# Spectral mixing with a gated feed-forward on one core: moving a group of transfers from the sync engine to GpSimd, and one sum into a DMA

## The chip, the cores and the metric

The kernel runs on one core of a Trainium2 chip. TensorE (PE in the profile) multiplies; VectorE (DVE) and ScalarE (ACT) do elementwise work; GpSimd (POOL) and SyncE (SP) issue transfers here; 16 DMA engines move the data. Each engine runs its own instructions in order and waits on semaphores for the others. The metric is the device time of one execution in microseconds; for comparing two kernels the median of several runs is used.

## The reference

With xn the layer-normalised x (2048 tokens, 512 features), two things are computed and joined:

```
a = xn @ dft_hid_re.T;  b = xn @ dft_hid_im.T           # [2048, 512]
s = dft_seq_re @ a - dft_seq_im @ b                     # [2048, 512]
h = xn @ w1 + b1;  h = max(h, 0) ** 2                   # [2048, 1792]
g = silu(h @ w2 + b2)
out = x + s * g
```

All in float32. The two hidden DFT matrices are 512 x 512, the two sequence matrices 2048 x 2048.

## The kernel before, in words

**Arithmetic.** Every operand is split into a high part, which TensorE takes in its fast float32 format (F32R), and a low part, the rest. A product is three passes: high x high, high x low, low x high. `split_hi` (L138) is done on ScalarE, `split_lo` (L141) on VectorE. Larger products use a scheme of seven block products in place of eight (`PRODUCTS`), for which sums and differences of the four blocks of an operand are needed. An operand with its sums has seven blocks, in a high and a low part.

**Sequence part.** The sequence DFT is done first, on xn itself: two products, P and Q, of xn with the sequence matrices, in eight chunks c of 256 output tokens. The first chunk (L410) is done without the scheme while x is still being normalised, and so is the first tile of the second chunk, j = 4 (`MIXED`, `plain_step`). All other tiles go through `steps`: first (1, 1), (1, 0), (1, 3), (1, 2), (1, 5), (1, 6), (1, 7), then eight tiles j for each of the chunks 2 to 7. A step is 42 products on TensorE (L399). For a later step, `step_load` (L291) loads a raw tile of the sequence matrices, 512 KB in four blocks, into one of three buffers u; `step_sums` makes four more blocks of it on VectorE (`sums_b`: one addition of two blocks at L305, then one block each at L311 and L312); `step_split` splits seven blocks into the buffer ga or gb (by the parity of j). The load for the step after next but two is issued when its buffer u comes free.

For the first step's tile, (1, 1), the addition of L305 is not done on VectorE: the loop over the first chunk loads the two blocks a second time into the place of the sum (L594) and lets GpSimd issue an accumulating DMA that adds the third block to both (L595). `step_sums` then does only L311 and L312 (`sums_b_rest`).

xn needs the same sums, in place in its tiles xn32, for two groups of four tiles (`sums`, L270): three subtractions on VectorE for a whole group (L275) and, for each tile, one accumulating DMA of GpSimd (L278). `split_sums` puts the result into the operands XC (tile xc) just ahead of the steps that use them, in the order 1, 0, 3, 2, 5, 6, 7, 4.

**Work beside the steps.** When a chunk is done, `closing` combines its seven accumulators into a tile e (c in the transfers' names), and at the steps j = 3 and 4 of the following chunk P and Q are stored to DRAM (PQD, L667). The table `EARLY` lists by step what else is done: seven weights' jobs (`weight`: d0 to d3 for the hidden DFT, v0, v1 and v6 for blocks of w1). A job loads a raw weight into pq00 (L449), makes its sums in pq01, splits them and stores the seven blocks, high and low, to DRAM in two transfers (L462, to WDD or W1D). Four jobs `load_wd` (p1, p0, p3, p2 in that order) load the hidden DFT's operands back into SBUF when room is free there, each in two halves, high then low (L513, tile wdp). P and Q are read back by `y_load` and `y_early` (L469).

**Hidden part and the rest.** From WDP and the operands of P and Q, eight units (YUnit, tiles r_A to r_D, L807) make s; then w1 (HUnit, L807) and w2 (L913, tiles m_o and m_last), and at last the gate and the output.

**Queues.** The program's order is written out by hand; each engine follows it. Nearly all transfers, loads and stores, are issued by SP in one queue (q1 in the profile). ScalarE issues the stores of s and h (q10). GpSimd issues 16 accumulating transfers (q0): the one of L595, eight of L278, and seven of L951 in the last part, which add x to the output. An issue waits for its semaphores on the issuing engine, and what is behind it on that engine waits too.

Of the kernel before, what the change touches and what calls it, by code (L numbers as in the profile page):

```python
# [8 lines left out]
F32 = mybir.dt.float32  # L9
# [123 lines left out]
def fnet_gated_kernel(ctx, tc, x, xt, ct, wd, w1, w2, b1, b2, out):  # L133
    nc = tc.nc
    ctx.enter_context(tc.manual_schedule(engines=None))

    def split_hi(hi, lo, src):
        nc.scalar.activation(hi, src, AF.Copy)  # L138
# [4 lines left out]
    def split(*parts):  # L143
        split_hi(*parts)
        split_lo(*parts)

    def copy(to, src, scale=1.0):
        nc.scalar.activation(to, src, AF.Copy, scale=scale)
# [12 lines left out]
    PQD = [dram.tile([P, 2, 4, 256], F32, name=f"pqd{c}") for c in range(NC)]  # L161
    WDD = [dram.tile([P, 2, 7, 256], F32, name=f"wdd{n}") for n in range(ND)]
# [9 lines left out]
    def buf(tag, shape, name, dtype=F32):  # L172
        return pool.tile(shape, dtype, tag=tag, bufs=3 if tag == "u" else 1, name=name)
# [96 lines left out]
    def sums(g):  # L270


        s = xn32[ND * g, "tile"].rearrange("p j h (b n) -> p j (h b) n", b=2)
        for to, a, b in ((3, 1, 3), (1, 1, 0), (0, 3, 0)):
            nc.vector.tensor_tensor(s[:, :, to], s[:, :, a], s[:, :, b], op=ALU.subtract)  # L275
            yield
        for j in (1, 0, 3, 2):
            nc.gpsimd.dma_start(s[:, j, 2], s[:, j, 0], accum_op=ALU.add)  # L278
        yield

# [4 lines left out]
    raw, part = {}, {}  # L285
# [60 lines left out]
    def step_sums(n):  # L346
        if n < len(steps):
            u = raw[steps[n]]
            (sums_b if n else sums_b_rest)(u[:, 4:8], u)

    def step_split(n):
        if n < len(steps):
# [79 lines left out]
    steps = [(1, j) for j in SEVEN] + [(c, j) for c in range(2, NC) for j in range(NJ)]  # L432
    order = [(0, j) for j in range(NJ)] + [(1, j) for j in MIXED] + steps
# [12 lines left out]
    def weight(n, raw_, sums_, to, k, turn=False):  # L446

        r = buf("pq00", [P, 4, 256], f"{n}r")
        nc.sync.dma_start(r, raw_)  # L449
        yield  # L450
        t = buf("pq01", [P, 4, 256], f"{n}t")
        if turn:
            copy(r[:, I22:I21 + 1], r[:, I22:I21 + 1], -1.0)
        first = sums_(t, r)
        next(first)
        yield
        list(first)
        yield
        g = buf(f"wd{int(k)}", [P, 2, 7, 256], f"{n}g", F32R)
        for q, src in ((slice(0, 3), r[:, 1:4]), (slice(3, 7), t)):  # L460
            split(g[:, HI, q], g[:, LO, q], src)
            nc.sync.dma_start(to[:, :, q], g[:, :, q].bitcast(F32))  # L462
            yield

    makers["d"] = lambda n: weight(f"wd{n}", wd[n], sums_b_steps, WDD[n], n % 2, True)
# [43 lines left out]
    def load_wd(n):  # L509
        t = operand_buf(("wd0", "wd1", "xc2", "xc1")[n], f"wdp{n}", 0)  # L510
        WDP[n] = t
        for i in range(2):
            nc.sync.dma_start(t[:, i].bitcast(F32), WDD[n][:, i])  # L513
            yield

    makers["y"] = y_early
# [42 lines left out]
    g = plain_parts(0, 1)  # L559
# [10 lines left out]
    for j in range(1, NJ):  # L570
        ln_rstd(j)
        if j == 1:
            ln_hi(j, 0)
            ln_shift(j)
            ln_xn_act(j, 0)
            ln_mean(j + 1, 1)
            split_lo(*plain_parts(0, j, one))
            ln_xn(j, 1)
            split_hi(*xc_parts(j, 1))
            split_lo(*xc_parts(j, 0))  # L580
            split_lo(*plain_parts(0, j, two))
        else:
            if j == NJ - 1:
                ln_shift(j)
                next(side[0])
            for h in range(2):
                (ln_xn_act if j == NJ - 1 else ln_xn)(j, h)
                split_hi(*xc_parts(j, h))
            split_lo(*g)
            split_lo(*xc_parts(j, 0))  # L590
        load_c(*order[j + 3])
        if order[j + 3] == steps[0]:
            u, (a, b) = raw[steps[0]], steps[0]
            nc.sync.dma_start(u[:, 4:6], ct[a, b, :, 1:3])  # L594
            nc.gpsimd.dma_start(u[:, 4:6], ct[a, b, :, 0:1].to_broadcast([P, 2, 256]), accum_op=ALU.add)  # L595
        if j in (1, 3, 4):
            load_x({1: 5, 3: 6, 4: 7}[j])
        if j + 1 < NJ:
            ln_stats(j + 1)
            if j > 1:  # L600
                ln_mean(j + 1, 1)
            ln_var(j + 1, 1)
            ln_root(j + 1)
        split_lo(*xc_parts(j, 1))
        if j == NJ - 1:
            some(side[0], 3)
        for h in range(2):
            products(j, h)
        g = plain_parts(*order[j + 1])
        split_hi(*g)  # L610
        if j == 2:
            nc.sync.dma_start(b1s, b1)
            nc.sync.dma_start(b2s, bcast(b2, D))
# [28 lines left out]
    for n, s in enumerate(steps):  # L642
        c, j = s
        if c > 1 and j == 0:
            ms = {}
        for k, tag in banks(c).items():
            if k not in ms:
                ms[k] = bank(tag, f"m{k}_{c}")
        g = part.pop(s)
        for p in FIRST if j == 0 and c > 1 else ORDER:  # L650
            a, b = PRODUCTS[p]
            mm(ms[p], XC[j][:, a], lambda b_: g[:, b_, b], (c > 1 and j == 0) or (not n and p in (1, 5, 6, 7)), s in LAST)
        step_sums(n + 2)
        step_split(n + 1)
        if n == 1:
            some(side[1], 2)
        if n in SUMS_AT:
            split_sums(SUMS_AT[n])
        if n == 0:
            e = buf("e", [P, 2048], "c1")  # L660
            copy(chunk_part(e)(C22), halves(ms[Z]))
        step_load(n + 4)
        if closing:
            some(closing, (LATER_1 if c == 2 else LATER).get(j, 0))
            if j in (3, 4):
                q = slice((j - 3) * 1024, (j - 2) * 1024)
                nc.sync.dma_start(PQD[c - 1][:, j - 3].rearrange("p k n -> p (k n)"), e[:, q])  # L667
            if j == 4:
                closing = None
        if s in LAST:  # L670
            if c > 1:
                e = buf("e", [P, 2048], f"c{c}")
            room = {}
            if c < NC - 1:
                room = buf("pq10", [P, 2, 512], f"left{c}")
                room = {7: room[:, 0], 5: room[:, 1], 3: buf("pq11", [P, 512], f"left3_{c}")}
            closing = closing_of(chunk_part(e), ms, room, c == 1)
            some(closing, 2)
        if s == (2, 4):
            nc.vector.transpose(stats_t, stats.rearrange("p m h j -> p (m h j)"))  # L680
            for q in range(4):
                nc.sync.dma_start(rows[:, q * 32:(q + 1) * 32], stats_t[q * 32:(q + 1) * 32, :])
        go(*EARLY.get(s, ()))
# [326 lines left out]
    for u in range(2, NC):  # L1010
        n = 2 * u + 2
# [83 lines left out]
    for n in range(NTC * NP):  # L1095
        c, p = divmod(n, NP)
# [37 lines left out]
        if p == NP - 1 and not last:  # L1134
            e = buf("e", [P, 4, 512], f"z{c}")
# [16 lines left out]
    e = buf("u", [P, 4, 512], f"z{c}")  # L1152
# [95 lines left out]
```

## Time and profile before

| | |
|---|---|
| median of 3 runs | 671.49 us (670.09 to 671.98) |
| the profiled execution, in all | 673.18 us |
| its span, first to last instruction | 671.4 us |
| ScalarE busy | 385.0 us, 57% |
| granted TensorE clock, mean | 0.996 |
| HBM read, written | 102.51 MB, 47.99 MB |
| transfers in SP's queue q1 | 129.54 MB |
| transfers in GpSimd's queue q0 | 3.15 MB |

The profile is of one execution; its times are in us from the span's start. A row of the timeline or of the chain gives start, duration, engine, line, operation and tiles (out<-in), then how many instructions are merged, and in brackets the idle time before them and what ended it. A name like SPq or POOLq is an engine's sequencer, which issues or waits. A row of the waits gives who waited for whom, then the total in us, the number of times and the longest. The row of a line gives the least, the median and the greatest duration in ns, and for DMAs "to landing" is the time from issue to the last byte in us. Matmuls overlap, so the duration of a single one is longer than the distance to the next.

### The profile page before, as it was taken

The page shows a single profiled execution, that of the slowest core. Times are in us where ns is not written, and L with a number is a line of the kernel's source. Part 1 is how long each engine was busy: PE and PEld are TensorE (multiplying, and loading weights), DVE is VectorE, ACT ScalarE, POOL GpSimd, SP SyncE. Part 2 cuts the span into 40 slices and gives each one's busy share as a digit, 9 for nine tenths or more (in the row PEclk, how much of TensorE's full clock was granted, in tenths as well). Part 3 has the DMA queues.
Part 4 walks back from the last instruction along what each step waited for, and adds up shares of the span by engine and source line. Part 5 has one row for each costly group of instructions (what it writes and reads, how often), then busy time and mean ns, then how long its engine had stood idle before and what let it go on. Part 6 is the DMA issues. An engine that isn't in the chain of part 4 may idle for free.

```text
span 671.4 us, 13549 instructions
## 1 busy us (share of the span) xinstructions
PE 662.7 (99%) x5587; PEld 651.3 (97%) x5587; DVE 611.2 (91%) x849; ACT 385.0 (57%) x518; POOL 17.2 (3%) x20
## 2 busy tenths in 40 slices
PE   8999999999999999999999999999999999999997
PEld 5889999999999999999999999999999999999997
DVE  7999999899999999999899988977877889999997
ACT  6866563544545354444465557788778865454451
POOL 0011200000000000000000000000000000101010
PEclk8999999999999999999999999999999999999999
DMA  8746634767587785869588558575755866777665
GB/s 284 233 126 188 162 120 151 249 233 258 197 290 268 244 297 176 301 237 337 194 305 275 185 189 310 196 263 206 271 182 197 326 243 207 197 216 198 212 204 156
DMA packets 54172, 152.41 MB, mean 227 GB/s; under 512 B 5216, under 2 KB 21088, under 8 KB 53472
## 3 DMA queue, kind: packets, MB, share of 16 engines
q1 hardware_dynamic: 44576, 129.54, 57.1%
q10 hardware_dynamic: 6208, 18.88, 7.1%
q0 software_dynamic: 3328, 3.15, 3.2%
q8 instruction: 43, 0.70, 0.4%
q14 instruction: 17, 0.14, 0.1%
HBM read 102.51 MB, written 47.99 MB: 224 GB/s over the span
## 4 chain that ended last, share of the span: by engine, by line
PE 90%; DVE 6%; DMA 2%; ACT 1%; issue 1%; SPq 0%; DVEq 0%; ACTq 0%
PE m L399 34%; PE m_o L913 15%; PE r_B L807 13%; PE r_A L807 9%; PE pq_b L410 5%; PE r_C L807 4%; PE r_D L807 4%; PE m_last L913 4%; DVE g L141 2%; PE pq_bb L410 2%; DMA u<-in_ct 1%; DMA x<-in_x 1%; DVE u L305 1%; DVE c L384 1%; ACT g L138 1%
## 5 line engine op out<-in xcount | busy, mean ns | idle before, releaser
L399 PEld LDWEIGHTS m<-g,xc 128*128 128x128 f32 x2358 | 268.9, 188 | 1.8 <-DVE g L141 1.5
L399 PE MATMUL m<-g,xc 128*128 128x256 f32 x2358 | 269.3, 277 | 1.3 <-DVE g L141 1.3
L138 ACT ACTIVATE g<-u 128x1792 fp32r<-128x1792 f32 (+2 forms) x65 | 103.6, 1593 | 132.5 <-PE m L399 92.6
L141 DVE TENSOR_TENSOR g<-u,g 128x1792 fp32r<-128x1792 f32 (+2 forms) x66 | 122.4, 1855 | 5.8 <-ACT g L138 5.3
L913 PE MATMUL m_o<-w,g 128*128 128x256 f32 x882 | 100.5, 276 | 0.0
L913 PEld LDWEIGHTS m_o<-w,g 128*128 128x128 f32 x882 | 100.3, 188 | 0.0
L138 ACT ACTIVATE g<-hr 128x1792 fp32r<-128x1792 f32 (+2 forms) x31 | 48.2, 1566 | 39.9 <-PE m_o L913 16.8
L807 PE MATMUL r_B<-xT,w 128*128 128x256 f32 x504 | 66.5, 276 | 0.0
L807 PEld LDWEIGHTS r_B<-xT,w 128*128 128x128 f32 x504 | 61.5, 188 | 0.0
L141 DVE TENSOR_TENSOR g<-hr,g 128x1792 fp32r<-128x1792 f32 (+2 forms) x31 | 56.7, 1838 | 3.0 <-ACT g L138 2.8
L410 PE MATMUL pq_b<-g,xc 128*128 128x512 f32 x144 | 42.1, 400 | 2.0 <-DVE small L249 2.0
L807 PE MATMUL r_A<-xT,w 128*128 128x256 f32 x336 | 43.1, 276 | 0.0
L807 PEld LDWEIGHTS r_A<-xT,w 128*128 128x128 f32 x336 | 40.3, 188 | 0.2 <-DVE xT L141 0.2
L305 DVE TENSOR_TENSOR u<-u 128x512 f32<-128x512 f32 x54 | 37.0, 685 | 2.4 <-DMA u<-in_ct 2.3
L410 PEld LDWEIGHTS pq_b<-g,xc 128*128 128x128 f32 x144 | 27.8, 194 | 8.4 <-ACT g L138 2.4
L807 PE MATMUL r_B<-wdp,yg 128*128 128x256 f32 x288 | 35.8, 276 | 0.0
L807 PEld LDWEIGHTS r_B<-wdp,yg 128*128 128x128 f32 x288 | 34.1, 188 | 0.0
L913 PE MATMUL m_last<-w,g 128*128 128x256 f32 x294 | 33.5, 276 | 0.0
L913 PEld LDWEIGHTS m_last<-w,g 128*128 128x128 f32 x294 | 33.4, 188 | 0.0
L141 DVE TENSOR_TENSOR yg<-yraw,yg 128x1792 fp32r<-128x1792 f32 x13 | 26.2, 2018 | 1.0 <-ACT yg L138 1.0
L138 ACT ACTIVATE yg<-yraw 128x1792 fp32r<-128x1792 f32 x13 | 22.2, 1708 | 5.5 <-DVE yraw L323 4.5
L312 DVE TENSOR_TENSOR u<-u 128x256 f32<-128x256 f32 x55 | 23.4, 425 | 1.9
(187 smaller groups left out, 843.8 us busy)
## 6 DMA issues: line engine op xcount, KB each, us to landing
u<-in_ct SPq DMA_DIRECT2D x63, 512.0 KB, 3.9
hd<-h ACTq DMA_DIRECT2D x28, 512.0 KB, 3.9
hr<-hd SPq DMA_DIRECT2D x28, 512.0 KB, 3.7
wdp<-wdd SPq DMA_DIRECT2D x8, 896.0 KB, 5.8
yraw<-pqd SPq DMA_DIRECT2D x13, 512.0 KB, 5.7
pqd<-c SPq DMA_DIRECT2D x12, 512.0 KB, 6.0
w<-w1d SPq DMA_DIRECT2D x6, 896.0 KB, 7.6
y<-y ACTq DMA_DIRECT2D x8, 512.0 KB, 5.0
```

The source lines that it names most:

```text
L138: nc.scalar.activation(hi, src, AF.Copy)
L141: nc.vector.tensor_tensor(lo, src, hi.bitcast(F32), op=ALU.subtract)
L305: nc.vector.tensor_tensor(t[:, 0:2], r[:, 0:1].to_broadcast([P, 2, 256]), r[:, 1:3], op=ALU.add)
L312: nc.vector.tensor_tensor(t[:, 3], t[:, 2], r[:, 3], op=ALU.add)
L384: nc.vector.tensor_tensor(part_(to), halves(room.get(m, ms[m])), part_(frm), op=op)
L399: nc.tensor.matmul(ps[:, d], w[:, a_, d * P:(d + 1) * P], halves(mv(b_)), start=first and d == 0 and (a_, b_) == (HI, HI), stop=last and ( ...
L410: nc.tensor.matmul(accs[k], w, part[0, j][:, b_, 2 * h:2 * h + 2], start=j == 0 and h == 0 and (a_, b_) == (HI, HI), stop=j == NJ - 1 and ...
L807: nc.tensor.matmul(self.region(REGION[k]), w, mv, start=i == 0 and k in (1, 7), stop=i == len(ops) - 1, skip_group_check=True)
L913: nc.tensor.matmul(m[:, i * 256:(i + 1) * 256], ready[n][:, a_, H_SLOT[a], i * P:(i + 1) * P], W2[p][:, b_, b], start=p == 0 and i == 0 an ...
```

## The change

Four issues are put on GpSimd in place of SP: the load of a raw weight (L449), the two stores of a job (L462), the reloads of the hidden DFT's operands (L513), and the stores of P and Q of the second to seventh chunk (L667). The stores of the first chunk's and of the last chunk's P and Q stay on SP.

The second step's tile, (1, 0), gets its first sum in the way that the first has it: a second load of two blocks on SP and an accumulating DMA on GpSimd, right behind its own load; VectorE's addition at L305 falls away for it.

In the second group of `sums` the four accumulating DMAs are issued for tiles 5, 6, 7, 4 in place of 5, 4, 7, 6.

```diff
-        for j in (1, 0, 3, 2):
+        for j in ((1, 0, 3, 2), (1, 2, 3, 0))[g]:
             nc.gpsimd.dma_start(s[:, j, 2], s[:, j, 0], accum_op=ALU.add)
...
-            (sums_b if n else sums_b_rest)(u[:, 4:8], u)
+            (sums_b if n > 1 else sums_b_rest)(u[:, 4:8], u)
...
-        nc.sync.dma_start(r, raw_)
+        nc.gpsimd.dma_start(r, raw_)
...
-            nc.sync.dma_start(to[:, :, q], g[:, :, q].bitcast(F32))
+            nc.gpsimd.dma_start(to[:, :, q], g[:, :, q].bitcast(F32))
...
-            nc.sync.dma_start(t[:, i].bitcast(F32), WDD[n][:, i])
+            nc.gpsimd.dma_start(t[:, i].bitcast(F32), WDD[n][:, i])
...
-        if order[j + 3] == steps[0]:
-            u, (a, b) = raw[steps[0]], steps[0]
+        if order[j + 3] in steps[:2]:
+            a, b = order[j + 3]
+            u = raw[a, b]
             nc.sync.dma_start(u[:, 4:6], ct[a, b, :, 1:3])
             nc.gpsimd.dma_start(u[:, 4:6], ct[a, b, :, 0:1].to_broadcast([P, 2, 256]), accum_op=ALU.add)
...
-                nc.sync.dma_start(PQD[c - 1][:, j - 3].rearrange("p k n -> p (k n)"), e[:, q])
+                nc.gpsimd.dma_start(PQD[c - 1][:, j - 3].rearrange("p k n -> p (k n)"), e[:, q])
```

## The prediction

> **What bounds the kernel now.** I read the page first, then the idle time of TensorE (the waits of engine PE), then the chain that ended last, then the timelines of SP, VectorE and GpSimd around the places that those named.
>
> ```profile
> span 671.4 us, 13549 instructions
> PE 662.7 (99%) x5587; PEld 651.3 (97%) x5587; DVE 611.2 (91%) x849; ACT 385.0 (57%) x518; POOL 17.2 (3%) x20
> ...
> PE pq_b L410 <- DVE small L249: 2.0, 1, 2.0
> PE m L399 <- DVE g L141: 1.3, 1, 1.3
> PE warm L537 <- DVE idle L533: 1.2, 1, 1.2
> ```
>
> TensorE is busy for all but 8.7 us of the span. Its waits are three. Two of them (2.0 and 1.2 us) lie before the first product, which the change does not reach. The third, 1.3 us, is the only one in the middle, and it is all that this change can win on TensorE. The chain shows how it arises:
>
> ```profile
> 117.00 7.61 DMA u<-in_ct
> 124.63 0.70 DVE u L305
> 126.15 2.03 DVE g L141
> 128.22 195.62 PE m L399 x1721
> ```
>
> A load of a raw sequence tile (u, 512 KB) is issued at 117.00 and takes 7.61 us; VectorE sums it, splits it, and TensorE can go on at 128.22. From there it runs without a stop for 195.62 us. Why that load was slow stands in SP's timeline, and in the landing times of SP's loads in the same stretch (the line view's answers for L291 from 53 to 322 us and for L449 at 114 us) and of VectorE's longest waits for a load:
>
> ```profile
> 112.07 0.33 SPq L291 DMA_DIRECT2D u<-in_ct  x1
> 112.67 0.33 SPq L667 DMA_DIRECT2D pqd<-c  x1
> 113.54 0.61 SPq L462 DMA_DIRECT2D wdd<-wd0g  x1
> 114.20 0.78 SPq L449 DMA_DIRECT2D wd1r<-in_wd  x1
> 117.00 0.33 SPq L291 DMA_DIRECT2D u<-in_ct  x1
> ...
> DMA to landing us min/median/max: 3.4/4.0/7.6
> ...
> DMA to landing us min/median/max: 9.1/9.1/9.1
> ...
> DVE u L305 <- DMA u<-in_ct: 2.3, 2, 1.7
> ```
>
> A u load alone lands in 3.4 us. At 112.67 to 114.20 SP put 512 KB of P/Q, 768 KB of a weight's store and 512 KB of the next raw weight into the same queue. The last of these landed at 114.20 + 9.1 = 123.3, and the u load behind it 1.3 us later, at 124.6: it stood in line. All 52 u loads of the stretch made VectorE wait only twice, 2.3 us together, both here.
>
> **The change part by part.** *(1) The moved issues.* Seven weights' jobs load once and store twice (21), four reloads have two halves (8), six chunks store P and Q twice (12): 41 DMAs go from SP's queue to GpSimd's. GpSimd's present issues bound the cost of one: 0.856 us at the least for 128 rows, 1.343 us for 256 rows.
>
> ```profile
> L278 POOL DMA_DIRECT2D xn<-xn x8: 856/1052/1562, 49.6 to 73.0; - x8
> ...
> DMA to landing us min/median/max: 3.0/4.1/5.9
> ...
> L595 POOL DMA_DIRECT2D u<-in_ct x1: 1343/1343/1343, 44.1 to 44.1; - x1
> ...
> DMA to landing us min/median/max: 5.9/5.9/5.9
> ...
> L951 POOL DMA_DIRECT2D z<-in_x x7: 1213/1222/1227, 575.2 to 660.4; - x7
> ...
> DMA to landing us min/median/max: 4.2/4.7/6.8
> ```
>
> 27 x 0.86 + 14 x 1.34 = 42 us, spread from 74 to 311 us over an engine that is busy 17.2 us in all and has nothing else there: no cost in itself. The waits go along in the old order (a store waits for its split, the next raw weight stands behind that store), so behind a waiting GpSimd instruction there are only other moved transfers.
>
> ```profile
> 121.74 1.22 DVE L141 TENSOR_TENSOR wd0g<-wd0t,wd0g 128x1024 fp32r<-128x1024 f32 x1
> ...
> 123.74 0.61 ACT L148 ACTIVATE wd1r<-wd1r 128x512 f32<-128x512 f32 x1
> 126.89 1.70 ACT L138 ACTIVATE g<-u 128x1792 fp32r<-128x1792 f32 x1 [2.54 <-PE m L399]
> ```
>
> The first to be needed soon is the raw weight of 114.20, which ScalarE reads at 123.7 and which landed 0.4 us before; two or three issues of about 1 us ahead of it and a shared engine may make it 1 to 2 us later. ScalarE then idles about 2.5 us before its next split at 126.89, so up to that it is hidden; beyond it each us is paid. I take 0.
>
> What it wins: the u load of 117.00 is now behind no store. Between "alone" (3.4, landing 120.4) and "as before" (124.6) I take half of the engines' rate: the 512 KB take about 1.3 us alone (the distance of the two landings at 123.3 and 124.6), so 3.4 + 1.3 = 4.7, landing 121.7. VectorE comes to it after its split at 121.74 + 1.2 = 122.9, and the 1.7 us wait is gone. The earlier wait, 0.6 us, may stay, since that load stood ahead of the stores. TensorE's 1.3 us needs 1.3 of the 1.7: **-1.3 us**; ends -1.3 and 0.
>
> By the Trainium skill (DMA: Bandwidth & Descriptors, "Issuing engines are not separate DMA queues") transfers of all issuing engines end on the same 16 DMA engines and interleave, and issuing from several saves only the issue time. SP's issue time is on no path here, so by that sentence alone this term would be 0. No run here shows two full streams on the two queues yet.
>
> *(2) The second tile's first sum.* It takes one VectorE addition away (L305, 0.68 us at 52.30), and adds a 256 KB load on SP and an accumulating DMA on GpSimd, for which the next sum (L311) then waits. The first tile does this already:
>
> ```profile
> 39.29 0.33 SPq L291 DMA_DIRECT2D u<-in_ct  x1
> 39.67 0.42 SPq L594 DMA_DIRECT2D u<-in_ct  x1
> ...
> 44.13 1.34 POOL L595 DMA_DIRECT2D u<-in_ct  x1 [43.68 <-DMA u<-in_ct]
> 44.73 6.07 SPq L291 DMA_DIRECT2D u<-in_ct  x2
> ...
> 52.30 0.68 DVE L305 TENSOR_TENSOR u<-u 128x512 f32<-128x512 f32 x1
> 53.02 0.43 DVE L311 TENSOR_TENSOR u<-u 128x256 f32<-128x256 f32 x1
> ...
> 60.66 2.02 DVE L141 TENSOR_TENSOR g<-u,g 128x1792 fp32r<-128x1792 f32 x1 [0.82 <-ACT g L138]
> ...
> 68.51 1.22 DVE L141 TENSOR_TENSOR xc<-xn,xc 128x1024 fp32r<-128x1024 f32 x1
> ...
> 53.23 27.00 PE L399 MATMUL m<-g,xc 128*128 128x256 f32 x232
> ...
> 55.98 1.06 ACT L138 ACTIVATE xc<-xn 128x1024 fp32r<-128x1024 f32 x1
> ```
>
> There the pair was issued at 39.29 and 39.67, and GpSimd could accumulate 4.46 us after the second, at 44.13. The second tile's own load goes out at 44.73 (when its buffer comes free), so its pair is at 45.1, the accumulating DMA at 45.1 + 4.46 = 49.6, and with the 5.9 us of the first it lands at 55.4. (The other 256 KB accumulations take 4.2 to 6.8: 53.8 to 56.4.) VectorE would be ready for L311 at 52.3 and waits 3.1 us. What is queued behind it there: L312, a sum of the rows (L275), the split of the first tile, the splits of the rows' sums (xc). From L311 at 53.02 to the end of the xc split at 69.73 VectorE idles 0.82 us at 60.66 and otherwise next to nothing (I take 1.0 in all), so its work is 16.7 - 1.0 = 15.7 us, and from 55.4 it ends at 71.1 instead of 69.7. TensorE needs that xc then: from 53.23 on it goes 0.1137 us a product (195.62 us for 1721 in the chain), 48 products of the mixed tile, 42 each of two steps and 14 of the third make 146, which is 69.8. There is no slack, and what is late is paid: **+1.4 us**. Ends: landing at 53.8 nothing, landing at 56.4 +2.4. I take 1.4, since the first tile's accumulation had the same neighbour, a u load issued 0.6 us behind it.
>
> GpSimd's own queue: the four accumulations into the rows (L278, from 49.62) now stand behind the second tile's, some 1 us later; ScalarE reads the first of them at 55.98, and its landing may now follow that of the tile, near 56. VectorE is late by more than that there. The changed order of the second group (L278 from 69.19) only puts them in the order in which they are split: nothing.
>
> *(3) The end of the sequence part.* The last weight reload is moved too, and its slack is small:
>
> ```profile
> 304.60 0.99 SPq L667 DMA_DIRECT2D pqd<-c  x1
> ...
> L513 SPq DMA_DIRECT2D wdp<-wdd x1: 526/526/526, 310.6 to 310.6; - x1
> ...
> DMA to landing us min/median/max: 11.9/11.9/11.9
> ...
> 323.68 1.52 PE L807 MATMUL r_A<-wdp,yg 128*128 128x256 f32 x12
> ```
>
> It landed at 310.6 + 11.9 = 322.5; its low part is first read by the eighth product, at 323.68 + 7 x 0.1137 = 324.5. From 304.6 on the GpSimd queue would carry two P/Q stores and two reload halves, 2 x 512 + 2 x 896 = 2816 KB, beside up to five P/Q loads of 512 KB, 2560 KB, that SP issues meanwhile. In line, as before, three of these stood ahead, and the reload came out after 2816 + 1536 = 4352 KB in the 16 us from about 306.5: 272 KB a us. If the queues take turns packet by packet, with 7 KB rows against 4 KB, 2816 KB go beside about 2050 KB, which is 4870 / 272 = 17.9 us, so 324.4. That is just in time: 0, with 1.8 us at the other end (all 5376 KB first, 326.3).
>
> **The sum** is -1.3 + 1.4 + 0 = +0.1 us. Against the profiled execution's own 673.18 us (span 671.4, 1.8 us outside it) that is 673.3; that execution lies 1.7 us over the median of the runs, so I add the difference to the median: 671.49 + 0.1 = **671.6 us**.
>
> **The rivals.** *The sum lands in time.* If the accumulation lands by 54.0, only -1.3 is left: 670.2. For it: 4.2 is the least of the seven later ones. Against it: the neighbouring load. *The u load is no earlier*, because the moved transfers, in flight at the same time, take as much of the engines from it as they did in line, and the sum is late: 671.49 + 1.4 = 672.9. For it: the bytes are the same, 1792 KB between 112.67 and 114.20. Against it: 123.3 and 124.6, one behind the other, with 1.3 us for the load's own bytes. The Trainium skill's sentence on issuing engines, above, would have it so. *Slower: the software queue is slow for large transfers,* at the end of the sequence part. Its accumulations need 3.0 us at the least for 128 KB and 4.2 for 256 KB, so 107 KB a us as a lower bound of the rate. TensorE is stopped at 324.5 if the 2816 KB pass at less than 2816 / 18 = 156 KB a us. At 130, between, they need 21.7 us, until 328.2: 3.7 us, giving 671.6 + 3.7 = 675.3. Against it: accumulating reads its target as well, a plain copy does not.
>
> **How the numbers follow.** About 0.3% (2.0 us) is what a measurement of this kernel can tell from no change. Chances: the forecast 0.50, the sum in time 0.20, no earlier load 0.15, the slow queue 0.12, something not seen 0.03. The first three lie within 0.3%; being faster by over 2.0 us would need more than all of the 1.3 us and is left with 0.05. Slower by over 2.0 us has the slow queue and the upper end of the late sum without the gain (671.49 + 2.4 = 673.9): 0.16. The range goes from 669.7 (the gain alone, less half a us of spread) to 674.4 (that upper end plus the same).
>
> **What would show it.** Right: no PE wait at 126 to 128; u loads between 112 and 125 landing in under 5.5 us; VectorE waiting 2 to 4 us before L311 near 52, released by the accumulating DMA; a PE wait near 59 and 70, together 1.4 us; the products with wdp following without a gap. Wrong: no wait at L311, a remaining wait near 128, or PE waiting at 324. The prediction fails if GpSimd's issues of plain transfers last several us each, or if ScalarE waits for a raw weight.

## The result and the profile after

The kernel after takes 677.78 us (median of 4 runs, 676.66 to 679.87), the kernel before in the same session 670.89 (4 runs, 670.09 to 671.98): ratio 1.0105, 95% interval 1.0074 to 1.0136, so 7 us slower. The forecast was 671.6 in a range of 669.7 to 674.4.

From L594 on, the lines of the kernel after are numbered one higher (L596 for L595, L668 for L667, L808 for L807). The page of the profiled execution after (677.24 us in all), busy time, one queue (packets, MB, share of 16 engines) and one group of transfers (KB each, median us to landing):

```profile
span 675.4 us, 13576 instructions
...
PE 664.5 (98%) x5587; PEld 651.5 (96%) x5587; DVE 609.6 (90%) x848; ACT 385.1 (57%) x518; POOL 42.6 (6%) x62
...
q0 software_dynamic: 10400, 33.56, 15.5%
...
wdp<-wdd POOLq DMA_DIRECT2D x8, 896.0 KB, 8.2
```

The work is as announced: GpSimd issues 42 transfers more (62 for 20), 25.4 us more of its time (42.6 for 17.2), and its queue carries 33.56 MB for 3.15. No engine has become the bound. What has grown is waiting. TensorE's and VectorE's waits of the kernel after (who waited for whom: us in all, times, longest):

```profile
PE m L399 <- DVE g L141: 4.4, 4, 1.4
...
DVE u L305 <- DMA u<-in_ct: 7.1, 4, 2.4
DVE u L311 <- DMA u<-in_ct: 3.7, 2, 2.6
```

Before, TensorE stood once in the middle, 1.3 us, and VectorE waited 2.3 us at L305. Now TensorE stands four times and VectorE waits 10.8 us for u tiles. The chain that ended last names the loads (start, us, what):

```profile
49.79 4.33 DMA u<-in_ct
...
116.84 7.65 DMA u<-in_ct
...
209.31 7.29 DMA u<-in_ct
...
234.39 7.86 DMA u<-in_ct
```

Four DMAs lie in the chain. The first is the new accumulation, the second the u load that was late before (7.61 then, 7.65 now: it gained nothing), the third and fourth are u loads that were not late before (4.49 and 6.05 us in the second profile of the kernel before).

For a comparison from end to end I use a second profile of the kernel before (first experiment; span 670.3), because in the first one TensorE's granted clock was 0.50 from 7.74 to 11.15 us. TensorE's timeline (start, us, products, and in brackets the stop ahead of them), kernel before, second profile:

```profile
127.18 195.67 PE L399 MATMUL m<-g,xc 128*128 128x256 f32 x1721 [1.37 <-DVE g L141]
```

and the kernel after:

```profile
58.15 68.59 PE L399 MATMUL m<-g,xc 128*128 128x256 f32 x588 [1.29 <-DVE g L141]
128.11 91.35 PE L399 MATMUL m<-g,xc 128*128 128x256 f32 x798 [1.37 <-DVE g L141]
220.22 24.68 PE L399 MATMUL m<-g,xc 128*128 128x256 f32 x210 [0.77 <-DVE g L141]
245.88 82.07 PE L399 MATMUL m<-g,xc 128*128 128x256 f32 x713 [0.97 <-DVE g L141]
```

The same 1721 products now lie in three rows. Their stops give 0.77 + 0.97 = 1.74 us. But the rows themselves are longer too: 91.35 + 24.68 + 82.07 = 198.10 for 195.67, 2.43 us more without a stop at which the view splits a row (some 0.3 of it is the end of a last product, counted three times for once). The new stop at 58.15 adds 1.29 us, and 0.60 us more is lost up to the stop at 128, which is the same in both. On the other side, the kernel after began these steps 0.96 us sooner (51.13 for 52.09). That makes 5.10 us, as much as the spans differ by. The medians differ by 6.9 us; what is left of that is not in these two executions. So the loss has two visible kinds: stops behind a late u load, and a **creep**, losses in the rows between the stops.

About half of the creep here is a slower pace: TensorE goes through whole steps with its products further apart. From 281 to 298 us (stretch, its length, TensorE's busy time and products, granted clock, DMA share, GB/s), the kernel after and, second, the kernel before:

```profile
281.00:298.00 17.00, 17.00 (x147) 1.00 0.60 228
...
281.00:298.00 17.00, 17.00 (x153) 1.00 0.72 266
```

Taken product by product, the trace after has one start every 0.1178 us from 143 to 152 and from 280 to 299 us, and every 0.1133 us in most of the rest; the slow ones behind 128 us add up to about 1.3 us. The granted clock is given as 1.00 in both. Such stretches are not found only behind late loads: the kernel before has one from 68 to 93 us. What sets the pace stays open.

### The profile page after: what moved, and what is told of

Its sections match the earlier page's. It is cut to its first block, busy times and chain, and to the rows that moved or that the text cites. A ratio compares the mean times of both kernels' runs of the same rounds, so it can differ in the third digit from the quotient of the medians.

```text
span 675.4 us, 13576 instructions
## 1 busy us (share of the span) xinstructions
PE 664.5 (98%) x5587; PEld 651.5 (96%) x5587; DVE 609.6 (90%) x848; ACT 385.1 (57%) x518; POOL 42.6 (6%) x62
## 3 DMA queue, kind: packets, MB, share of 16 engines
q0 software_dynamic: 10400, 33.56, 15.5%
## 4 chain that ended last, share of the span: by engine, by line
PE 82%; DVE 10%; DMA 4%; ACT 2%; issue 1%; SPq 0%; DVEq 0%; ACTq 0%
PE m L399 27%; PE m_o L914 15%; PE r_B L808 13%; PE r_A L808 9%; PE r_C L808 4%; PE r_D L808 4%; DMA u<-in_ct 4%; DVE g L141 4%; PE pq_b L410 4%; PE m_last L914 4%; PE pq_bb L410 1%; ACT g L138 1%; DVE u L305 1%; DVE u L311 1%; DVE c L384 1%
## 5 line engine op out<-in xcount | busy, mean ns | idle before, releaser
L399 PE MATMUL m<-g,xc 128*128 128x256 f32 x2358 | 272.2, 277 | 4.6 <-DVE g L141 4.4
L399 PEld LDWEIGHTS m<-g,xc 128*128 128x128 f32 x2358 | 270.5, 188 | 6.4 <-DVE g L141 5.7
L808 PE MATMUL r_B<-xT,w 128*128 128x256 f32 x504 | 66.5, 276 | 0.0
L808 PEld LDWEIGHTS r_B<-xT,w 128*128 128x128 f32 x504 | 61.5, 188 | 0.0
L808 PE MATMUL r_A<-xT,w 128*128 128x256 f32 x336 | 43.1, 276 | 0.0
L305 DVE TENSOR_TENSOR u<-u 128x512 f32<-128x512 f32 x53 | 36.3, 684 | 7.2 <-DMA u<-in_ct 7.1
L410 PE MATMUL pq_b<-g,xc 128*128 128x512 f32 x144 | 41.1, 392 | 1.0 <-DVE small L249 1.0
L808 PEld LDWEIGHTS r_A<-xT,w 128*128 128x128 f32 x336 | 40.3, 188 | 0.2 <-DVE xT L141 0.2
L808 PE MATMUL r_B<-wdp,yg 128*128 128x256 f32 x288 | 35.8, 276 | 0.0
L808 PEld LDWEIGHTS r_B<-wdp,yg 128*128 128x128 f32 x288 | 34.1, 188 | 0.0
L410 PEld LDWEIGHTS pq_b<-g,xc 128*128 128x128 f32 x144 | 26.7, 188 | 7.6 <-ACT g L138 1.4
L952 POOL DMA_DIRECT2D z<-in_x x7 | 8.5, 1216 | 341.9 <-DVE z L964 301.5
L311 DVE TENSOR_TENSOR u<-u 128x256 f32<-128x256 f32 x55 | 23.4, 425 | 5.6 <-DMA u<-in_ct 3.7
```

The costliest lines, as they stand in the source:

```text
L305: nc.vector.tensor_tensor(t[:, 0:2], r[:, 0:1].to_broadcast([P, 2, 256]), r[:, 1:3], op=ALU.add)
L311: nc.vector.tensor_tensor(t[:, 2], t[:, 1], r[:, 1], op=ALU.add)
L399: nc.tensor.matmul(ps[:, d], w[:, a_, d * P:(d + 1) * P], halves(mv(b_)), start=first and d == 0 and (a_, b_) == (HI, HI), stop=last and ( ...
L410: nc.tensor.matmul(accs[k], w, part[0, j][:, b_, 2 * h:2 * h + 2], start=j == 0 and h == 0 and (a_, b_) == (HI, HI), stop=j == NJ - 1 and ...
L808: nc.tensor.matmul(self.region(REGION[k]), w, mv, start=i == 0 and k in (1, 7), stop=i == len(ops) - 1, skip_group_check=True)
L952: nc.gpsimd.dma_start(z, at(x[c * TC:(c + 1) * TC], k), accum_op=ALU.add)
```

## The experiments

Times are device us, the ratio is to the kernel before in the same session, with its 95% interval.

| kernel | us | ratio |
|---|---|---|
| after | 677.78 | 1.0105 (1.0074 to 1.0136) |
| the sum alone | 674.23 | 1.0052 (1.0033 to 1.0071) |
| the moves alone | 674.02 | 1.0053 (1.0039 to 1.0067) |
| after, reload on SP | 673.14 | 1.0039 (1.0023 to 1.0056) |
| before, one reload half earlier on SP | 672.01 | 1.0022 (1.0010 to 1.0033) |
| the reload alone, first set (4 of 5) | 676.83 | 1.0094 (1.0078 to 1.0110) |
| the reload alone, second set | 675.33 | 1.0067 (1.0053 to 1.0081) |
| the reload alone, paced | 673.00 | 1.0026 (1.0014 to 1.0038) |
| raw weights, their stores, P and Q alone | 671.91 | 1.0027 (1.0010 to 1.0043) |
| the same, d1's load a step later | 670.12 | 0.9993 (0.9982 to 1.0004) |
| before, d1's load a step later on SP | 669.57 | 0.9986 (0.9977 to 0.9994) |
| the sum alone, larger descriptor space | 672.77 | 1.0031 (1.0018 to 1.0045) |

**Theory A:** what counts is when a transfer goes out beside the u loads, not who issues it. **Rival B:** the second queue is slow, or takes its share from the first packet by packet. For the sum, **theory C:** the second accumulation is held back by GpSimd's descriptor space; **rival D:** GpSimd is simply busy.

### The kernel before, once more

No edit.

> The kernel before, unchanged, for a second profile. In the first one TensorE's clock was granted at half from 7.7 to 11.2 us and the first chunk began 2.2 us later than in the changed kernel, which had the full clock there. If that is a matter of the single execution, this profile may begin without it: first products of L410 at about 7.0 us instead of 7.8, span about 669, and the one wait near 126 of 1.3 us as before. If it belongs to the kernel before, the half clock is there again and the span is 671.4.

One execution, 672.07 us, span 670.3, between the two that were expected. The half clock was not there, and yet the first product of L410 came at 7.69 us, little sooner than the 7.83 of the first profile. TensorE's wait in the middle:

```profile
PE m L399 <- DVE g L141: 1.4, 1, 1.4
```

The stop in the middle is the same as in the first profile, so it belongs to the kernel; the half clock at the start does not. The chance for a gain was still one stop of 1.4 us.

### The sum alone, the moves alone

The first is the change without the four moved issues, the second only those:

```diff
-        nc.sync.dma_start(r, raw_)
+        nc.gpsimd.dma_start(r, raw_)
...
-            nc.sync.dma_start(to[:, :, q], g[:, :, q].bitcast(F32))
+            nc.gpsimd.dma_start(to[:, :, q], g[:, :, q].bitcast(F32))
...
-            nc.sync.dma_start(t[:, i].bitcast(F32), WDD[n][:, i])
+            nc.gpsimd.dma_start(t[:, i].bitcast(F32), WDD[n][:, i])
...
-                nc.sync.dma_start(PQD[c - 1][:, j - 3].rearrange("p k n -> p (k n)"), e[:, q])
+                nc.gpsimd.dma_start(PQD[c - 1][:, j - 3].rearrange("p k n -> p (k n)"), e[:, q])
```

> The second tile's first sum by accumulating DMA and the order of the second group, all transfers else on SP as before. Theory (the late sum costs by itself): VectorE waits 2.5 us or so for the accumulation before L311 near 54, TensorE waits 1.3 us near 57 and is 1.5 us late from there, the wait of 1.3 us near 127 stays, none near 219 and 244: about 1.5 us slower than before, 672.4. Rival (the late sum is caught up, since VectorE has 0.7 us less to do): same time as before, 670.9.

> The moved transfers without the second tile's sum. Theory (the moved transfers make u loads late): waits of TensorE near 127 (1.3), 219 (1) and 244 (1.2) as in the changed kernel and some small ones, none near 57: 4 to 5 us slower than before, about 675.5. Rival (the late sum is the main cost): within 1 us of before.

The sum alone costs 0.0052 x 671 = 3.5 us, the moves alone 3.6, together 7.1: all of the loss. Of the sum 1.5 us were expected, of the moves 4 to 5. These two halves add, but finer parts, below, do not. By the same reckoning the moves without the reload cost 1.8 us, and together with the sum, at 3.5, not 5.3 but 2.6; and the reload alone cost 4.5 to 6.3 us, more than all the moves with it. So a part's price holds only beside the parts with which it was measured. The sum alone, TensorE's and VectorE's waits:

```profile
PE m L399 <- DVE g L141: 2.4, 2, 1.2
...
DVE u L311 <- DMA u<-in_ct: 3.6, 2, 2.6
```

One of its two stops is the old one; the new one, 1.2 us at 58, is the late accumulation. VectorE's smaller wait at L311, 1.1 us (0.5 in the second profile of the kernel before), is for the first tile's accumulation, which took 6.29 us for 5.66. The moves alone had stops of 0.68 us at 126 and 0.80 us at 218, and none at 244, where one was expected. GpSimd's timeline:

```profile
204.04 0.70 POOL L462 DMA_DIRECT2D w1d<-w10g  x1 [8.79 <-DVE w10g L141]
204.63 0.68 POOL L449 DMA_DIRECT2D w11r<-in_w  x1
205.28 0.56 POOL L513 DMA_DIRECT2D wdp<-wdd  x1
```

The reload half of 205.28 goes out 1.8 us ahead of the u load of 207.12, which lands after 7.3 us. In the kernel before it stood on SP behind that load, which landed after 4.5 us:

```profile
208.08 0.33 SPq L291 DMA_DIRECT2D u<-in_ct  x1
208.63 0.33 SPq L513 DMA_DIRECT2D wdp<-wdd  x1
```

On SP the reload had to wait until the u load's buffer came free, though it had no need of that buffer itself. On GpSimd it waits for its own buffer and for the moved transfers ahead of it alone.

That is the first half of this reload, and the stop at 220. The second half, near the stop at 245, stood ahead of its u load on SP as well: 228.08 and 231.52 in the second profile of the kernel before, where that load took 6.05 us; 231.85 and 234.39 in the kernel after, where it took 7.86. Here the order is the old one. What differs is the time between the two, 2.5 us for 3.4, and the queue.

### After, with the reload back on SP

```diff
-            nc.gpsimd.dma_start(t[:, i].bitcast(F32), WDD[n][:, i])
+            nc.sync.dma_start(t[:, i].bitcast(F32), WDD[n][:, i])
```

> The changed kernel with the reloads of the hidden DFT's operands (L513) issued by SP again. Theory 1 (engines serve transfers in the order of issue over both queues, and GpSimd issues the reload halves ahead of a u load that SP used to put first): the waits near 219 and 244 vanish, those near 57 and 127 stay, 2 to 3 us faster than the changed kernel, about 675. Theory 2 (the software queue itself carries large transfers slowly, stores and raw weights too): the waits near 219 and 244 stay at least by half, since the stores of w1 and of P and Q and the raw weights are still there; at most 1 us faster, about 677.

677.78 becomes 673.14, a larger gain than the 2 to 3 us of theory 1. The waits of TensorE in this kernel:

```profile
PE m L399 <- DVE g L141: 2.0, 2, 1.6
```

The two left are the sum's at 59 (1.59 us) and the old one at 127 (0.45 us); those at 220 and 245 are gone. Beside the other moves and the sum, the reload was more than half of the loss.

### One reload half a step earlier, still on SP

```diff
-    (4, 2): ("d3", "v0"), (4, 4): ("d3",), (4, 5): ("v0",), (4, 6): ("v0", "v0", "v1"), (4, 7): ("p1",), (5, 1): ("v0",),
+    (4, 2): ("d3", "v0"), (4, 4): ("d3",), (4, 5): ("v0",), (4, 6): ("v0", "v0", "v1", "p1"), (5, 1): ("v0",),
```

> The kernel before, all on SP, but with the first half of the second reload (p1) listed one step earlier, so that SP issues it right behind the raw weight near 206 and ahead of the u load near 208, as GpSimd does in the changed kernel. Theory 1 (what counts is the order of issue, whichever queue): that u load lands in 7 us or more instead of 4.5, VectorE waits about 2 us for it near 215, TensorE about 1 us near 217; 1 to 1.5 us slower than before, 672.1. Theory 2 (the software queue is what is slow): no wait there, time as before, 670.9.

(p1 is called the second by its number; it is the first of the four to run.) This makes GpSimd's order on SP's queue: the reload at 204.78, the u load behind it at 207.57. That load's landing, and TensorE's row behind the old stop:

```profile
DMA to landing us min/median/max: 5.6/5.6/5.6
...
125.63 197.77 PE L399 MATMUL m<-g,xc 128*128 128x256 f32 x1721 [1.10 <-DVE g L141]
```

5.6 us for 4.5, and the 1721 products take 197.77 for 195.67: 2.1 us of creep, 1.3 us in the medians. Much of it is the slower pace, from 222 to 256 us. The landing grew less than expected (7 us or more), and the stop of 1 us near 217 did not come. But a loss is there without any second queue. That speaks for A; it does not yet rule out that a second queue costs something on top. On SP the reload went out 2.8 us ahead of the u load, on GpSimd 1.8, and this 1 us explains less than the 1.7 us between landings of 5.6 and 7.3.

### The reload alone on GpSimd

Only L513 is changed, in the kernel before.

> The kernel before with the reloads of the hidden DFT's operands alone (L513) issued by GpSimd. Theory 1 (order of issue): GpSimd has nothing else there and issues each half as soon as its buffer is free and its stores have landed, ahead of u loads; waits of TensorE near 217 to 245 of 1 to 2 us in all; 672.5 to 674. Rival (it needs the stores and raw weights in the same software queue to be late): within 0.5 us of before.

1.0094: a miss, and dearer than all the moves together. One of its five executions, the profiled one, took 1360.32 us, with TensorE at half its usual pace throughout (551.02 us for 2358 products), and is left out. The second set is of the same kernel:

> The reload of the split weights alone is issued by GpSimd, everything else as before; taken again for a trace at full clock. Theory A (what counts is when a transfer goes out, and GpSimd lets the reload go out ahead of the u load that it stood behind on the sync engine): a time of 675.5 to 678, the two halves of the first reload on their way before the u loads of their steps, u loads of 7 us and more near 207 and 234 where the kernel before has 4.5 to 6, and stalls of TensorE near 219 and 246 of 2 us together and more, with a creep of small losses behind them. Rival B (the second queue itself is slow or takes its share from the first, packet by packet): the same time, but the u loads are slower in every stretch in which a reload runs, whichever of the two was issued first, those near 320 included.

1.0067. GpSimd's timeline and TensorE's:

```profile
201.58 1.10 POOL L513 DMA_DIRECT2D wdp<-wdd  x2 [129.61 <-DMA wdd<-wd3g]
```

```profile
208.12 9.84 PE L399 MATMUL m<-g,xc 128*128 128x256 f32 x84 [0.44 <-DVE g L141]
218.88 91.32 PE L399 MATMUL m<-g,xc 128*128 128x256 f32 x798 [0.91 <-DVE g L141]
310.49 5.05 PE L399 MATMUL m<-g,xc 128*128 128x256 f32 x42 [0.29 <-DVE g L141]
316.17 9.69 PE L399 MATMUL m<-g,xc 128*128 128x256 f32 x83 [0.63 <-DVE g L141]
```

Here GpSimd has nothing else to do, and both halves go out at once at 201.58, as soon as their buffer is free: the job d3 has it until its last store (wdd<-wd3g in the brackets) has landed. In the moves alone a weight's store ahead of them on GpSimd had waited for VectorE until 204.04, and that paced them by accident. The u loads around them took 6.8 and 7.2 us (issued 201.93 and 208.10), and the stops follow at 208 and 218; the place of the second half, 228 in the kernel before, is now free, and there is no stop at 245. The stops are where the reload goes out: those at 310 and 316 follow four halves issued from 296.17 to 301.46, beside which two u loads took 7.0 and 8.1 us. The one expected at 246 was wrong for that reason.

### The reload alone, paced

GpSimd copies one column of the u tile whose load was issued last, ahead of seven of the eight halves (the lines are numbered one higher here, L400 for L399):

```diff
+            if now[0] + 4 < len(steps):
+                nc.gpsimd.tensor_copy(stats_t[:, 0:1], raw[steps[now[0] + 4]][:, 0, 0:1])
             nc.gpsimd.dma_start(t[:, i].bitcast(F32), WDD[n][:, i])
```

> As the kernel with only the reload on GpSimd, but ahead of seven of the eight reload halves GpSimd copies one column of the u tile whose load was issued last at that step, into a tile that is no longer used, so that the reload can't go out before that u load has landed; queue, bytes and engine of the reload stay. Theory A (order and time of issue): the loss of the reload on GpSimd goes, 670.5 to 672, u loads near 207 at 5.5 us and below, no stall of TensorE at 219 or 246. Rival B (the second queue): no better than without the copies, 675 to 678.

1.0026 for 1.0067 to 1.0094, intervals apart. The u loads from 200 to 213 us, and TensorE's timeline:

```profile
DMA to landing us min/median/max: 3.4/3.4/4.5
...
125.68 186.21 PE L400 MATMUL m<-g,xc 128*128 128x256 f32 x1638 [0.57 <-DVE g L141]
313.30 10.05 PE L400 MATMUL m<-g,xc 128*128 128x256 f32 x83 [1.41 <-DVE g L141]
```

Queue, engine and bytes are those of the reload alone, with small copies beside them; the time of issue is another (212.16 and 230.65 us for the first two halves), and both stops and creep are gone for 186 us (186.21 / 1638 = 0.1137 a product, as before). The second queue by itself is not the loss in this stretch. The time was expected at 670.5 to 672 and is 673.0: a new stop of 1.41 us stands at 313, where the copy let a half out at 301.34, 0.09 us ahead of a u load of 301.43 that then took 8.2 us. Pacing by the landing of one load puts the reload in front of the next.

### Raw weights, their stores, P and Q alone

The moves without L513.

> The kernel before with only the weights' raw loads, their stores and the stores of P and Q on GpSimd (no reload moved, no second sum). From the reload_back run, in which TensorE's wait near 127 was 0.7 instead of 1.6 us and none stood at 219: 0.5 to 1 us faster than before, 670.2. Rival (these moves cost as well, and the late sum is less than it seemed): 671 to 673.

671.91, slower where a gain was expected; the rival's 671 to 673 was right. The moved load of d1's raw weight and TensorE's row behind it:

```profile
112.11 0.65 POOL L449 DMA_DIRECT2D wd1r<-in_wd  x1
...
124.83 197.29 PE L399 MATMUL m<-g,xc 128*128 128x256 f32 x1721 [0.33 <-DVE g L141]
```

The stop near 124 shrinks to 0.33 us, and 197.29 for 195.67 says that more, 1.6 us, is lost again in creep. The u load of 114.58 lands 6.6 us later, 1.8 us behind the raw weight that was issued 2.5 us ahead of it on the other queue.

### The same, with d1's load one step later

```diff
-    (2, 0): ("d0",), (2, 2): ("d0",), (2, 3): ("d0", "d1"), (2, 5): ("d0",), (2, 6): ("d1", "d1"), (3, 0): ("d1", "d2"),
+    (2, 0): ("d0",), (2, 2): ("d0",), (2, 3): ("d0",), (2, 4): ("d1",), (2, 5): ("d0",), (2, 6): ("d1", "d1"), (3, 0): ("d1", "d2"),
```

> The kernel with the raw weights, their stores and the P and Q stores on GpSimd (671.9), and besides d1's raw weight load one step later, which in GpSimd's own order puts it behind the P/Q store of that step. Theory A (the DMA engines serve both queues in the order of issue, so the u load on the sync engine's queue stood behind the raw weight load on the other): the raw load goes out near 116 in its place of 112.1, behind the u load of 114.6, which then lands near 119.8 (5.2 us) in its place of 121.2 (6.6); VectorE's wait of 1.4 us at L305 near 121 goes, and the time is 670.8 to 671.5. Rival B (the queues share the DMA engines packet by packet, so which of the two goes out first counts little): the u load still takes 6.3 us and more, and the time stays at 671.7 to 672.2.

GpSimd's timeline, the u load of 114.17, and TensorE's timeline:

```profile
115.10 0.56 POOL L668 DMA_DIRECT2D pqd<-c  x1 [3.30 <-DVE stats_t L681]
115.73 0.53 POOL L449 DMA_DIRECT2D wd1r<-in_wd  x1
...
DMA to landing us min/median/max: 4.9/4.9/4.9
...
91.04 147.28 PE L399 MATMUL m<-g,xc 128*128 128x256 f32 x1297 [0.21 <-DVE c L384]
239.23 81.13 PE L399 MATMUL m<-g,xc 128*128 128x256 f32 x713 [0.91 <-DVE g L141]
```

The raw weight now goes out behind the u load, and that load takes 4.9 us in place of 6.6, on the same two queues with the same bytes. The old stop is gone, and so is the creep (147.28 / 1297 = 0.1136). 670.12, below what A expected, and 0.9993 with an interval that holds 1. For this u load A holds and B falls.

For another load of the same kernel B does not fall. The stop of 0.91 us at 239 is new, and the kernel before has none there. It follows the u load of 227.81 (chain), ahead of which stand a reload half on SP and a store of P or Q on GpSimd (timeline):

```profile
223.76 0.43 SPq L513 DMA_DIRECT2D wdp<-wdd  x1
224.36 0.55 POOL L668 DMA_DIRECT2D pqd<-c  x1 [8.02 <-DVE c L384]
...
227.81 7.79 DMA u<-in_ct
```

In the second profile of the kernel before the same two transfers, both on SP, went out 3.4 to 3.8 us ahead of this load (here 3.4 to 4.1), and its landing took less:

```profile
DMA to landing us min/median/max: 6.1/6.1/6.1
```

The other traces bear this out. With the reload half ahead of it and P and Q stored by SP, this load took 5.8 to 6.1 us in six profiles (before, before once more, the sum alone in both forms, one reload half earlier, d1 later on SP); with P and Q stored by GpSimd, 6.8 to 7.9 us in five (after, the moves alone, reload back on SP, and the two of this kind). The next store of P or Q, issued just behind this load, landed 1.3 us behind it on SP's queue and 0.2 to 1.1 us behind it on GpSimd's. That speaks for B here: the second queue takes some of this load's share. So it is not shown that the moves are free once d1 is in its place. In this trace they cost a stop of 0.91 us, and the later d1 pays for it; the next kernel, which has the later d1 without the moves, is at 0.9986, with an interval that overlaps.

### The kernel before, with d1's load one step later on SP

The same line of the table, nothing else.

> The kernel before, all on SP, with the raw weight of the second job (d1) loaded one step later, so that SP issues it behind the u load near 117 instead of ahead of it. Theory 1 (transfers stand in line in the order of issue): that u load lands about 1.3 us earlier, near 122.3 in place of 123.6, VectorE's wait of 1.7 us for it falls to under 0.5, and TensorE's wait near 126 of 1.5 us to under 0.3; 1.2 us faster, 669.7. Rival (the stores ahead of it set the landing, not the raw weight): same as before.

TensorE's timeline:

```profile
51.27 268.97 PE L399 MATMUL m<-g,xc 128*128 128x256 f32 x2358
```

There is no stop that the view shows in the whole stretch, the u load near 115 takes 5.7 us in place of 7.7, and VectorE's waits at L305 come down to 0.8 us. 669.57, ratio 0.9986 (0.9977 to 0.9994): the fastest of all, though by less than the 0.3% that the prediction called measurable. The prize that the change was after can be had by one entry of a table, and it is about 1 us.

### The sum alone, with twice the descriptor space

```diff
-    nc = bacc.Bacc("TRN2", target_bir_lowering=False, num_devices=1, dynamic_dma_scratch_size=1024)
+    nc = bacc.Bacc("TRN2", target_bir_lowering=False, num_devices=1, dynamic_dma_scratch_size=2048)
...
-    b2s = pool.tile([P, D], F32, name="b2s")
+    b2s = pool.tile([P, 256], F32, name="b2s")
...
```

The edits of the sum are in it as well. The kernel leaves out the second half of b2 and adds the first half in its place, so its output is not that of the reference, and its load, near 20 us, is half as large.

> The kernel with the second tile's accumulating sum alone, with GpSimd's descriptor space doubled (2048 for 1024); the room for it comes from holding b2 256 wide, so the second half of b2 is replaced by its first half in the output. Theory C (the second accumulation goes out only when the first has landed, since its descriptors don't fit beside those of the first): the second is issued as soon as its load has landed, near 48.4 to 49.0 where it was 49.8, and the other accumulations no longer 0.25 to 0.30 us behind the landing of one before; it lands 0.8 us sooner, VectorE waits 1.7 to 2 at L311 in its place of 2.6, and the time is 673.2 to 673.9 (674.2 without). Rival D (it is the engine that generates descriptors that is busy): issued at 49.8 as before and no change in the time.

GpSimd's timeline of the sum alone:

```profile
43.27 1.33 POOL L596 DMA_DIRECT2D u<-in_ct  x1 [42.83 <-DMA u<-in_ct]
49.82 1.23 POOL L596 DMA_DIRECT2D u<-in_ct  x1 [5.22 <-issue]
50.55 1.45 POOL L278 DMA_DIRECT2D xn<-xn  x1
54.39 2.65 POOL L278 DMA_DIRECT2D xn<-xn  x3 [2.39 <-issue]
```

and with the larger space:

```profile
48.57 1.21 POOL L596 DMA_DIRECT2D u<-in_ct  x1 [4.11 <-DVE g L141]
49.30 4.09 POOL L278 DMA_DIRECT2D xn<-xn  x4
```

"Issue" means a wait for nothing that the profile shows. In the sum alone the second accumulation's own load had landed at 48.30 (issued 44.03, 4.3 us), but it went out at 49.82, 0.26 us after the first had landed (43.27 + 6.29 = 49.56). With the larger space it goes out at 48.57, 0.53 us after its load (48.04), and the four L278 follow without a gap. D falls: the engine was not busy, it was out of space. But the other half of C missed: the accumulation lands after 5.6 us in place of 4.3, at 54.12 as before (48.57 + 5.55, and 49.82 + 4.31 = 54.13), and VectorE waits 2.8 us at L311. A u load of 512 KB goes out at 48.34 to 48.53 ahead of it in both kernels; it lands 2.1 to 2.4 us sooner than the accumulation. With the larger space four accumulations of L278 also go out close behind, in place of one. Which of these sets the landing is not tested. The time still fell, to 672.77, below what C expected: 1.0052 to 1.0031, with intervals that overlap, from two sessions. TensorE's rows behind the old stop, the sum alone first:

```profile
127.85 196.76 PE L399 MATMUL m<-g,xc 128*128 128x256 f32 x1721 [1.21 <-DVE g L141]
```

and with the larger space:

```profile
127.67 195.62 PE L399 MATMUL m<-g,xc 128*128 128x256 f32 x1721 [0.57 <-DVE g L141]
```

The creep of 1.1 us is gone there; in the sum alone it was the slower pace, from 143 to 152 and from 167 to 182 us. Whether accumulations that were held back until 54.39 can cause that so much later, or whether it differs from execution to execution, stays open.

## Why the prediction was wrong, by its steps

**What bounds the kernel, and the most that can be won: right.** Removing the one stop was worth at most 1.3; the kernel without any stop is 1 us faster.

**(1) The moved issues, -1.3: this step failed.** It measured +3.6 (the moves alone). Two of its terms were wrong.

The first is the gain. "I take half of the engines' rate" gave the u load near 117 a landing after 4.7 us, on a queue without stores. In the kernel after it landed behind the same raw weight as ever, which now was on the other queue: 123.20 and 124.49 (before: 123.3 and 124.6). The kernel after, landing times of the raw weight issued at 114.38 and the u load issued at 116.84:

```profile
DMA to landing us min/median/max: 8.8/8.8/8.8
...
DMA to landing us min/median/max: 7.7/7.7/7.7
```

The rival "no earlier load" had this landing right, with a chance of 0.15, though not the time. The Trainium skill (DMA: Bandwidth & Descriptors, "Issuing engines are not separate DMA queues") says that issuing from several engines saves only the issue time, and the trace of the kernel after agrees: 7.61 us before, 7.65 after. In three other kernels with these moves the load took 6.6 to 7.0 us and TensorE's stop behind it was 0.33 to 0.68 us, so there a part of the 1.3 us was won, and lost again elsewhere. The Trainium skill (the same page, "Queues, rings and completion order") says that a DMA engine takes turns between its queues packet by packet. The runs show that the order of issue counts beside that: near 115 the u load took 6.6 us issued behind the raw weight on the other queue, and 4.9 ahead of it; but near 230 it took 6.8 to 7.9 us with P and Q on the other queue and 5.8 to 6.1 without, in nearly the same order.

The second is the cost. The moved issues have "no cost in itself. The waits go along in the old order": true on GpSimd, whose time is off every path (25.4 us more, not the 42 of the estimate). But the order between the two engines went. I counted what would wait on GpSimd, and not what each transfer had waited for on SP: the u load ahead of it, whose buffer must come free. That wait had kept the first half of the reload behind the u load. That only two of 52 u loads made VectorE wait I read as slack. Loads of 7.3 and 7.9 us in place of 4.5 and 6.1 stop TensorE at 220 and 245; the first by the order, the second with the order as it was, by a shorter distance and the second queue.

**(2) The sum, +1.4: the wait was right, the place and the size were not.** Expected issue 49.6, landing 55.4, VectorE waiting 3.1 us at L311, TensorE 1.4 near 59 and 70. Measured 49.79, 54.12, 2.6, and 1.29 at 58 alone. That 1.29 lies near 1.4 is luck: with 15.7 us of VectorE's work behind it and a need at 69.8, the prediction's own sum makes a landing at 54.12 cost nothing. The stop came at another need, the split of the first tile. VectorE ended it at 58.10, and TensorE wanted it at 56.86, since it began its steps at 51.13. In the first profile it had begun them at 53.23, behind the half clock, and the same need lay near 59.0, so the prediction, which worked from 53.23, saw no stop there. As a term the sum measured 3.5: 1.2 the stop, 1.1 the creep behind 127 (196.76 us for the 1721 products, for 195.67), if that belongs to it; the rest I can't place. That GpSimd held the accumulation back until the first had landed was not foreseen; 49.6 came out near by another reason.

**(3) The last reload, 0: right.** It landed at 314.64 + 11.80 = 326.44, and the first products with wdp follow without a stop at 327.78, the whole stretch being later. The rival "slow software queue" did not come as a stop there, though the halves of 896 KB landed after 8.2 us (median) and after 5.8 before.

**The range** was short because no case had a price for a u load made late by a transfer that left sooner. The stops at 220 and 245 (1.74 us) had no term, and neither had the creep, which was larger (2.4 us behind 127).

## What to carry to other kernels

A transfer's place in an engine's program is a timing device: before moving its issue to another engine, write down what it waits for where it stands now, the issues ahead of it included, and ask when it will go out without them. Where transfers compete with a load that is just in time, move the issue behind that load before trying another queue; here one step in a table won what the second queue could not. Where two engines are nearly full, don't take the sum of the stops for the loss: compare the length of rows of equal products as well. And take slack from more than one profile before a forecast rests on it.

## What was not expected of the hardware

- Transfers of SP's and GpSimd's queues landed nearly in the order of issue: 2.5 us ahead on the other queue cost a 512 KB load 1.7 us (6.6 for 4.9).
- The second queue is not free either: with the stores of P and Q on it, the u load near 230 took 6.8 to 7.9 us (five profiles), with all on SP 5.8 to 6.1 us (six).
- With 1024 of descriptor space GpSimd issued a second accumulation of 256 KB only 0.26 us after the first had landed; with 2048 it issued it 0.53 us after its own load.
- GpSimd's issue of a plain transfer took 0.53 to 0.75 us, its issues of accumulations 0.86 us and more.
- TensorE went through whole steps of 42 products in 4.95 us and through most in 4.76, at a granted clock of 1.00 in both. Over the last 1721 products, in the sum alone, the raw weights with P and Q, the earlier reload half and after, that and short stops cost 1.1 to 2.4 us; the paced kernel and the two with d1's load later lost 0.4 us or less outside their stops. Whether a late load brings the slower pace about is not shown.
